# A fused linear attention and two-layer MLP on one core: the first weight tile loaded later, two chunks in the accumulators' banks, a state sum moved inside its half step, another order of the last two steps

## The chip, the core and the metric

The kernel runs on one core of a Trainium2 chip. Its time is the device time of one execution, in microseconds (us), from the launch to the last output byte. Three runs of the kernel before took 585.03, 585.46 and 587.11 us; the median, 585.46 us, is the time that the changed kernel is compared with. The names of the engines are those of the profile: PE multiplies matrices, PEld loads its weights, DVE and POOL work on tensors of elements, ACT computes functions, SP issues the DMA transfers.

## The reference

```python
gamma = 1.0 - 2.0 ** (-5.0 - np.arange(H))
for t in range(S):                       # linear attention, B=2, H=8, S=768, D=64
    state = gamma * state + k[:, :, t] outer v[:, :, t]
    y[:, :, t] = scale * q[:, :, t] @ state
x = y as (1536 tokens, 512)
h = x @ w_in;  g = max(h, 0) + alpha * min(h, 0);  x = g @ w_out       # 512 -> 2048 -> 512
h = x @ w_in2; P = a0 + a1 h + a2 h^2 + a3 h^3
Q = 1 + |b0||h| + |b1| h^2;  g = P / (Q + 1e-6);  out = g @ w_out2
```

Activations are float32, the weights are float64. All products of the MLPs are made of three matmuls of a high and a low half (x high by w high, x low by w high, x high by w low).

## The kernel before, in words

**Attention.** The 1536 tokens are 12 chunks of 128, c0 to c11, six for each batch. A chunk has two parts on PE. Its scores (`att_b`, L132, two PSUM banks sc0 and sc1) are masked on DVE into `s` (L136); `q` is scaled on ACT (L141) and, for chunks 0 to 3, on POOL (L143). Then `att_c` makes the output y of the chunk: y from `s` and v (L154), the new term of the state `st` (L166), and y from the old state R and q (L178); DVE adds `st` to R (L184), ACT and DVE split y into the halves xh (L188) and xl (L189), which are the input of the first MLP. Chunks 0 to 3 run ahead of the main loop, with 8 small matmuls (L498, two records each) ahead of the first of them; the scores of chunk 4 are behind them, and the rest of the chunks stand inside the main loop, at places that a table names (`stages`).

**MLPs.** 96 steps (`STEPS`) go over three blocks of 512 tokens and 16 tiles of 128 columns of the first and of the second MLP. Step i multiplies x by one tile of w_in (`pe_h`, L310, 12 matmuls, one PSUM bank) two steps ahead of the use, activates it, and multiplies the result by the tile of w_out into four accumulators (`pe_out`, L327, 12 matmuls). The first three products of step 0 are w high by g high, w high by g low, w low by g high.

**PSUM.** Four banks are a ring, given in turn to scores, to `h`, and to y and `st` of the chunks in the main loop (`rbank`). Four are the accumulators; the chunks ahead of the main loop use them for y and `st` (`abank`).

**Weights.** They arrive as raw 64-bit words, 512 KB a tile (L246), in the order of the list `SEQ`: k0, k1 and k2 are the first three tiles of w_in, k3 is the first tile of w_out, then they alternate. A tile is made into float32 by ACT (L254), three steps on DVE (L260, L264, L268), a cast to the high half on ACT (L279), and a subtraction to the low half on DVE (L285). `START` names the half step at which the first of these begins, and a helper, `half`, issues what falls due; at its end it issues the loads of the next tiles (`load_next`), as long as no more than 3 to 4 are under way. The half steps -12 to -5 belong to the chunks ahead of the loop, one each. `START[0,0,0]` is set by hand to -10, one earlier than the rule of its neighbours gives.

**Loads.** All loads go by SP, in program order, into one queue. Ahead of the loop: q and k transposed of a chunk (L102, L103) and k and v (L106, L107), 256 KB each; the first weight tile stands behind the first two chunks' q and k.

**The end.** In the second MLP the activation of a step is in four parts: `act2_front` (ACT: L372 to L374) and `act2_q` (DVE: L378), `act2_mid` (ACT: L385, L386; DVE: L387, L388), `act2_tail` (DVE: L396, L397, L400) and `act2_split` (ACT cast, L407; then L409). The order of the program is the order on each engine.

Of the kernel before, what the change touches and what calls it, by code (L numbers as in the profile page):

```python
# [21 lines left out]
LA = 2  # L22
NSTEP = 2 * NB * NF
QC = 1.0 + 1e-6
NWARM = 8
NSLOT = 42
GA = 5
GC = 10
# [3 lines left out]
def tile_fused(  # L32
# [18 lines left out]
    nc = tc.nc  # L51
# [49 lines left out]
    def load_kq(c):  # L101
        nc.sync.dma_start(out=att[c]["q"], in_=qT[c])  # L102
        nc.sync.dma_start(out=att[c]["t"], in_=kT[c])  # L103

    def load_nv(c):
        nc.sync.dma_start(out=att[c]["k"], in_=kn[c])  # L106
        nc.sync.dma_start(out=att[c]["v"], in_=vn[c])  # L107
# [37 lines left out]
    def att_c(c, ybank, pbank):  # L145
        a = att.pop(c)
        y = ybank(f"y{c}")
        first = c % CPB == 0
        last = c % CPB == CPB - 1
        for j in range(NK):  # L150
            js = slice(j * P, (j + 1) * P)
            for e in range(2):
                h = 2 * j + e
                nc.tensor.matmul(  # L154
                    y[64 * e:64 * e + 64, js],
                    a["v"][:, 64 * h:64 * h + 64],
                    a["s"][:, 512 * e + j * P:512 * e + (j + 1) * P],
                    start=(j == 0),
                    stop=(first and j == NK - 1),
                )  # L160
        if not last:
            pst = pbank(f"st{c}")
            for h in range(2 * NK):
                j, e = divmod(h, 2)
                hs = slice(64 * h, 64 * h + 64)
                nc.tensor.matmul(  # L166
                    pst[64 * e:64 * e + 64, 64 * j:64 * j + 64],
                    a["k"][:, hs],
                    a["v"][:, hs],
                    start=True,  # L170
                    stop=True,
                )
        if not first:
            for j in range(NK):
                js = slice(j * P, (j + 1) * P)
                for e in range(2):
                    es = slice(64 * e, 64 * e + 64)
                    nc.tensor.matmul(y[es, js], R[es, j, :], a["q"][es, js], start=False, stop=(j == NK - 1))  # L178
        if not last:
            src = pst[:, 0:256].rearrange("p (j d) -> p j d", j=NK)  # L180
            if first:
                nc.scalar.copy(R, src)
            else:
                nc.vector.tensor_tensor(out=R, in0=R, in1=src, op=ALU.add)  # L184
        b, o = divmod(c * P, TB)
        osl = slice(o, o + P)
        hap = xs(0, b, slice(0, 4), osl)
        nc.scalar.copy(hap, r4(y))  # L188
        nc.vector.tensor_tensor(  # L189
            out=xs(1, b, slice(0, 4), osl), in0=r4(y), in1=hap.bitcast(F32), op=ALU.subtract  # L190
        )
        for nm in ("qk", "kv", "s"):
            drop(a[nm])
# [27 lines left out]
    START = {}  # L221
    for m in A:
        START[0, m, 0], START[0, m, 1] = 2 * m - 9, 2 * m - 4
    START[0, 0, 0] = -10
    for j, m in enumerate(B):
        START[0, m, 0], START[0, m, 1] = 6 + (17 * j) // 5, 8 + (17 * j) // 5
    for m in range(NF):
# [12 lines left out]
    def load_next(depth):  # L240
        while loaded[0] < len(SEQ) and loaded[0] - loaded[1] < depth:
            k = loaded[0]
            loaded[0] += 1
            l, m, n = SEQ[k]
            r = alloc(f"r{k}", U32)
            nc.sync.dma_start(out=r, in_=SRC[l][n][m].bitcast(U32))  # L246
            words = r.rearrange("p (f t) -> p f t", t=2)
            raw[k] = (words[:, :, 0], words[:, :, 1], r)
# [106 lines left out]
    def act1_hi(i):  # L355
        nc.scalar.copy(g_tiles(i)[0], T1[i][1])  # L356

    def act1_lo(i):
        gh, gl = G[i]
        _, p, t = T1.pop(i)  # L360
        nc.vector.tensor_tensor(out=gl, in0=p, in1=gh.bitcast(F32), op=ALU.subtract)  # L361
        drop(t)
# [103 lines left out]
    def half(t, scalar_last=None, between=None):  # L466
        evs = dec.get(t, ())

        def each(nm):
            return [e[1] for e in evs if e[0] == nm]  # L470

        for e in each("abs"):
            w_abs(e)
        for e in each("hi"):
            w_hi(e)
        if scalar_last:
            scalar_last()
        for e in each("word"):
            w_word(e, 0)
        for e in each("lo"):  # L480
            w_lo(e)
        for e in each("word"):
            w_word(e, 1)
        if between:
            between()
        for e in each("word"):
            w_word(e, 2)
        if later and t % 2 == 0:
            split_x(*later.pop(0))
        load_next(3 if t < -6 else 4 if t < 2 * N1 else 2)  # L490

    with tc.manual_schedule():
        wt = alloc("wz")
        wz = wt[:, 0:P]
        nc.vector.memset(wz, 0.0)
        ps = rbank("warm")
        for _ in range(NWARM):
            nc.tensor.matmul(ps[:, 0:P], wz, wz, start=True, stop=True)  # L498
        nc.scalar.preload_act_table_set("natural_log_exp_and_others")
        for c in range(4):  # L500
            att_tiles(c)
        load_kq(0)
        nc.sync.dma_start(out=dm_sb, in_=dm)
        nc.sync.dma_start(out=cst_sb, in_=cst)
        load_nv(0)
        load_kq(1)
        load_next(1)
        load_kq(2)
        load_nv(1)
        nc.sync.dma_start(out=dq_sb, in_=dq)  # L510
        load_kq(3)
        load_nv(2)
        load_nv(3)
        load_next(3)
        nc.sync.dma_start(out=alpha_sb, in_=alpha)
        nc.sync.dma_start(out=ab_sb[:, 0:4], in_=pa.partition_broadcast(P))
        nc.sync.dma_start(out=ab_sb[:, 4:6], in_=pb.partition_broadcast(P))
        nc.vector.memset(bb_sb[:, 2:3], QC)

        def keep_warm(cnt):  # L520
            w = abank(3)("warm")
            for _ in range(cnt):
                nc.tensor.matmul(w[:, 0:P], wz, wz, start=True, stop=True)  # L523

        order = [("b", 0), ("c", 0), ("b", 1), ("b", 2), ("c", 1), ("b", 3), ("c", 2), ("c", 3)]
        for n, (s, c) in enumerate(order):
            if n in (1, 2, 3):
                keep_warm((3, 2, 3)[n - 1])
            if s == "b":
                att_k(c)  # L530
                att_b(c, rbank)
            else:
                att_c(c, abank(c % 2), abank(2 + c % 2))
                if c < 2:
                    att_load(4 + c)
            if n == 6:
                nc.scalar.activation(bb_sb[:, 0:2], ab_sb[:, 4:6], AF.Abs)
                nc.scalar.mul(nalpha_sb, alpha_sb, -1.0)
            half(n - NPRE)
        drop(wt)  # L540
        att_b(4, rbank)
        att_k(4)


        stages = {-4: ("c", 4)}
        for c, t, u in ((5, -3, -2), (6, -1, 1), (7, 2, 4), (8, 5, 6), (9, 7, 9), (10, 10, 12), (11, 13, 14)):
            stages[t] = ("b", c)
            stages[u] = ("c", c)

        def stage(t):  # L550
            if t not in stages:
                return
            s, c = stages[t]
            if s == "b":
                att_b(c, rbank)
                att_k(c)
            else:
                att_c(c, rbank, rbank)
                if c + 2 < NCH:
                    att_load(c + 2)  # L560
                if c == NCH - 1:
                    drop(dm_sb)

        for i in range(-LA, NSTEP):
            new, old = i + LA, i + LA - 1
            if new < NSTEP - 1:
                pe_h(new)
            if new == NSTEP - 2:
                pe_h(NSTEP - 1)
            if 0 <= old < N1:  # L570
                half(2 * i, lambda: act1_hi(old), lambda: act1_lo(old))
            else:
                if N1 <= old < NSTEP:
                    act2_tail(old)
                half(2 * i)
            if N1 <= new < NSTEP:
                act2_front(new)
                act2_q(new)
            if N1 <= old < NSTEP:
                act2_split(old)  # L580
            stage(2 * i)
            if i >= 0:
                pe_out(i)
            if i >= 0 and STEPS[i][4]:
                evac(i)
            if N1 <= new < NSTEP:
                act2_mid(new)
            stage(2 * i + 1)
            half(2 * i + 1, (lambda: act1_front(new)) if new < N1 else None)
            if new < N1:  # L590
                act1_join(new)
# [77 lines left out]
```

## Time and profile before

| | |
|---|---|
| median of three runs | 585.46 us |
| the profiled execution | 585.32 us |
| its span in the trace | 583.5 us |
| outside the span | 1.82 us |
| PE | 574.8 us busy, 99% |
| DVE | 466.3 us busy, 80% |
| ACT | 365.5 us busy, 63% |
| POOL | 76.0 us busy, 13% |

PE is busy in nearly the whole span, so what is left to gain is PE's idle time, and what can be lost is any wait that is put in front of PE. The 40 slices of the profile's page show it below full use in the first two and the last. The load queue is busy at the start: 327 to 401 GB/s in the first four slices (58 us), less than half of that afterwards.

### The profile page before, as it was taken

The page shows a single profiled execution, that of the slowest core. Times are in us where ns is not written, and L with a number is a line of the kernel's source. Part 1 is how long each engine was busy: PE and PEld are TensorE (multiplying, and loading weights), DVE is VectorE, ACT ScalarE, POOL GpSimd, SP SyncE. Part 2 cuts the span into 40 slices and gives each one's busy share as a digit, 9 for nine tenths or more (in the row PEclk, how much of TensorE's full clock was granted, in tenths as well). Part 3 has the DMA queues.
Part 4 walks back from the last instruction along what each step waited for, and adds up shares of the span by engine and source line. Part 5 has one row for each costly group of instructions (what it writes and reads, how often), then busy time and mean ns, then how long its engine had stood idle before and what let it go on. Part 6 is the DMA issues. An engine that isn't in the chain of part 4 may idle for free.

```text
span 583.5 us, 8093 instructions
## 1 busy us (share of the span) xinstructions
PE 574.8 (99%) x3040; PEld 474.6 (81%) x3040; DVE 466.3 (80%) x733; ACT 365.5 (63%) x663; POOL 76.0 (13%) x60
## 2 busy tenths in 40 slices
PE   9989999999999999999999999999999999999996
PEld 8768787888888888888888888888888888888885
DVE  3898687688684364548998999999998999887886
ACT  3676465556553453436765787777786786686672
POOL 2402000000000000000000312223222221221220
PEclk9999999999999999999999999999999999999999
DMA  9998422334321002012451011001111100010101
GB/s 327 340 401 326 145 73 73 109 109 145 108 73 36 1 37 73 36 38 90 176 204 37 0 37 37 23 15 37 36 38 37 38 0 1 0 73 2 63 9 74
DMA packets 18760, 50.65 MB, mean 87 GB/s; under 512 B 2592, under 2 KB 2592, under 8 KB 18720
## 3 DMA queue, kind: packets, MB, share of 16 engines
q1 hardware_dynamic: 18720, 50.13, 24.2%
q8 instruction: 24, 0.39, 0.3%
q14 instruction: 16, 0.13, 0.1%
HBM read 46.97 MB, written 3.15 MB: 86 GB/s over the span
## 4 chain that ended last, share of the span: by engine, by line
PE 93%; DVE 3%; ACT 2%; DMA 1%; issue 0%; ACTq 0%
PE h L310 44%; PE acc L327 43%; PE sc L132 2%; PE y L154 2%; PE y L178 1%; DMA qk<-in_qT_dram 1%; PE st L166 1%; PE warm L498 1%; DVE z L268 0%; DVE p L424 0%; PE warm L523 0%; ACT kv L120 0%; ACT g L407 0%; DVE as L400 0%; DVE z L264 0%
## 5 line engine op out<-in xcount | busy, mean ns | idle before, releaser
L310 PE MATMUL h<-xh,wh 128*128 128x512 f32 x384 | 150.3, 391 | 1.5 <-DVE xl L189 1.5
L310 PE MATMUL h<-xh,wl 128*128 128x512 f32 x384 | 149.5, 389 | 0.0
L310 PE MATMUL h<-xl,wh 128*128 128x512 f32 x384 | 149.4, 389 | 0.0
L327 PE MATMUL acc<-wh,g 128*128 128x512 f32 x384 | 125.9, 390 | 0.4 <-ACT g L407 0.4
L409 POOL TENSOR_TENSOR g<-as,g 128x512 fp32r<-128x512 f32 x46 | 63.4, 1378 | 447.9 <-PE acc L327 265.1
L327 PE MATMUL acc<-g,wh 128*128 128x512 f32 x384 | 118.9, 391 | 0.0
L310 PEld LDWEIGHTS h<-xh,wh 128*128 128x128 f32 x384 | 72.2, 188 | 17.3 <-DVE xl L189 1.7
L327 PEld LDWEIGHTS acc<-wh,g 128*128 128x128 f32 x384 | 72.0, 188 | 16.1 <-ACT g L407 0.8
L310 PEld LDWEIGHTS h<-xh,wl 128*128 128x128 f32 x384 | 72.1, 188 | 15.0
L327 PEld LDWEIGHTS acc<-g,wh 128*128 128x128 f32 x384 | 71.6, 188 | 15.6 <-issue 0.7
L310 PEld LDWEIGHTS h<-xl,wh 128*128 128x128 f32 x384 | 72.1, 188 | 14.6
L279 ACT CAST wh<-z 128x512 fp32r<-128x512 f32 x64 | 39.6, 619 | 58.4 <-DVE z L268 57.0
L327 PE MATMUL acc<-g,wl 128*128 128x512 f32 x192 | 74.7, 389 | 0.0
L327 PE MATMUL acc<-wl,g 128*128 128x512 f32 x192 | 74.7, 389 | 0.0
L351 DVE SCALAR_TENSOR_TENSOR np<-np,nalpha_sb 128x512 f32<-128x512 f32 x48 | 35.9, 748 | 39.9 <-ACT np L346 39.9
L345 ACT ACTIVATE np<-h 128x512 f32<-128x512 f32 x48 | 28.5, 594 | 45.3 <-PE h L310 45.3
L372 ACT ACTIVATE as<-h 128x512 f32<-128x512 f32 x48 | 28.6, 597 | 41.2 <-PE h L310 41.2
L378 DVE SCALAR_TENSOR_TENSOR as<-as,bb_sb,rr 128x512 f32<-128x512 f32 x48 | 37.9, 791 | 13.0 <-ACT rr L373 13.0
L361 DVE TENSOR_TENSOR g<-np,g 128x512 fp32r<-128x512 f32 x48 | 33.9, 707 | 17.4 <-ACT g L356 17.2
L268 DVE SCALAR_TENSOR_TENSOR z<-r,z 128x512 uint32<-128x512 uint32 x64 | 44.9, 701 | 1.5
L264 DVE SCALAR_TENSOR_TENSOR z<-r,z 128x512 uint32<-128x512 uint32 x64 | 44.9, 702 | 1.0
L285 DVE TENSOR_TENSOR wl<-z,wh 128x512 fp32r<-128x512 f32 x64 | 45.0, 703 | 0.1
(55 smaller groups left out, 748.3 us busy)
## 6 DMA issues: line engine op xcount, KB each, us to landing
r<-in_w1i_dram SPq DMA_DIRECT2D x16, 512.0 KB, 5.1
r<-in_w1o_dram SPq DMA_DIRECT2D x16, 512.0 KB, 3.8
r<-in_w2i_dram SPq DMA_DIRECT2D x16, 512.0 KB, 3.4
r<-in_w2o_dram SPq DMA_DIRECT2D x16, 512.0 KB, 3.2
qk<-in_qT_dram SPq DMA_DIRECT2D x12, 256.0 KB, 6.4
qk<-in_kT_dram SPq DMA_DIRECT2D x12, 256.0 KB, 6.4
kv<-in_kn_dram SPq DMA_DIRECT2D x12, 256.0 KB, 6.2
kv<-in_vn_dram SPq DMA_DIRECT2D x12, 256.0 KB, 6.5
```

Source lines behind the costliest of these rows:

```text
L264: nc.vector.scalar_tensor_tensor(out=zu, in0=lo, scalar=29, in1=zu, op0=ALU.logical_shift_right, op1=ALU.bitwise_or)
L268: nc.vector.scalar_tensor_tensor(out=zu, in0=hi, scalar=0x80000000, in1=zu, op0=ALU.bitwise_and, op1=ALU.bitwise_or)
L279: nc.scalar.copy(hi, Z[k])
L285: nc.vector.tensor_tensor(out=lo, in0=Z[k], in1=hi.bitcast(F32), op=ALU.subtract)
L310: nc.tensor.matmul(ps, w[:, ks], xs(hl, b, k, ALL), start=(n == 0), stop=(n == 11))
L327: nc.tensor.matmul(acc[0][k], a, c, start=(begin and n == 0), stop=(end != "" and n == 2))
L345: nc.scalar.activation(n, h, AF.Relu, scale=-1.0)
L351: nc.vector.scalar_tensor_tensor(out=p, in0=n, scalar=nalpha_sb[:, m:m + 1], in1=p, op0=ALU.mult, op1=ALU.add)
L361: nc.vector.tensor_tensor(out=gl, in0=p, in1=gh.bitcast(F32), op=ALU.subtract)
L372: nc.scalar.activation(s, h, AF.Square)
L378: nc.vector.scalar_tensor_tensor(out=s, in0=s, scalar=bb_sb[:, 1:2], in1=r, op0=ALU.mult, op1=ALU.add)
L409: eng.tensor_tensor(out=gl, in0=a, in1=gh.bitcast(F32), op=ALU.subtract)
```

## The change

It has six parts. (1) 7 of the small matmuls instead of 8. (2) The hand-set start of the first weight tile goes, so that its conversion begins one half step later, with chunk 1's output instead of the scores of chunk 2. (3) The loads ahead of the loop are in another order: the first weight tile behind chunk 2's k and v instead of behind chunk 1's q and k. (4) y and `st` of chunks 4 and 5 use the accumulators' banks. (5) The chunk work of an even half step (`stage(2 * i)`) is issued between the second and the third DVE step of the weight conversion instead of after the half step. (6) In the last step `act2_front` and `act2_q` of step 95 are issued ahead of `act2_tail` of step 94.

```diff
--- before.py
+++ after.py
@@ -22,7 +22,7 @@
 LA = 2
 NSTEP = 2 * NB * NF
 QC = 1.0 + 1e-6
-NWARM = 8
+NWARM = 7
 NSLOT = 42
 GA = 5
 GC = 10
@@ -221,7 +221,6 @@
     START = {}
     for m in A:
         START[0, m, 0], START[0, m, 1] = 2 * m - 9, 2 * m - 4
-    START[0, 0, 0] = -10
     for j, m in enumerate(B):
         START[0, m, 0], START[0, m, 1] = 6 + (17 * j) // 5, 8 + (17 * j) // 5
     for m in range(NF):
@@ -504,12 +503,12 @@
         nc.sync.dma_start(out=cst_sb, in_=cst)
         load_nv(0)
         load_kq(1)
+        load_nv(1)
+        load_kq(2)
+        nc.sync.dma_start(out=dq_sb, in_=dq)
+        load_nv(2)
         load_next(1)
-        load_kq(2)
-        load_nv(1)
-        nc.sync.dma_start(out=dq_sb, in_=dq)
         load_kq(3)
-        load_nv(2)
         load_nv(3)
         load_next(3)
         nc.sync.dma_start(out=alpha_sb, in_=alpha)
@@ -555,7 +554,10 @@
                 att_b(c, rbank)
                 att_k(c)
             else:
-                att_c(c, rbank, rbank)
+                if c < 6:
+                    att_c(c, abank(c % 2), abank(2 + c % 2))
+                else:
+                    att_c(c, rbank, rbank)
                 if c + 2 < NCH:
                     att_load(c + 2)
                 if c == NCH - 1:
@@ -567,18 +569,26 @@
                 pe_h(new)
             if new == NSTEP - 2:
                 pe_h(NSTEP - 1)
-            if 0 <= old < N1:
-                half(2 * i, lambda: act1_hi(old), lambda: act1_lo(old))
+            if old < N1:
+
+                def middle():
+                    if old >= 0:
+                        act1_lo(old)
+                    stage(2 * i)
+
+                half(2 * i, (lambda: act1_hi(old)) if old >= 0 else None, middle)
             else:
+                if new == NSTEP - 1:
+                    act2_front(new)
+                    act2_q(new)
                 if N1 <= old < NSTEP:
                     act2_tail(old)
                 half(2 * i)
-            if N1 <= new < NSTEP:
+            if N1 <= new < NSTEP - 1:
                 act2_front(new)
                 act2_q(new)
             if N1 <= old < NSTEP:
                 act2_split(old)
-            stage(2 * i)
             if i >= 0:
                 pe_out(i)
             if i >= 0 and STEPS[i][4]:
```

On SP, ahead of the loop: the four loads of chunk 4 (qk4, kv4), of chunk 5 (qk5, kv5) and the weight tiles r3 (k3, the first of w_out) and r4. Before:

```order
L106 DMA kv4_172<-in_kn_dram 128x512
L107 DMA kv4_172<-in_vn_dram 128x512
L246 DMA r3_227<-in_w1o_dram 128x1024
L102 DMA qk5_258<-in_qT_dram 128x512
L103 DMA qk5_258<-in_kT_dram 128x512
L106 DMA kv5_259<-in_kn_dram 128x512
L107 DMA kv5_259<-in_vn_dram 128x512
L246 DMA r4_319<-in_w1i_dram 128x1024
```

After:

```order
L106 DMA kv4_171<-in_kn_dram 128x512
L107 DMA kv4_171<-in_vn_dram 128x512
L102 DMA qk5_252<-in_qT_dram 128x512
L103 DMA qk5_252<-in_kT_dram 128x512
L106 DMA kv5_253<-in_kn_dram 128x512
L107 DMA kv5_253<-in_vn_dram 128x512
L245 DMA r3_261<-in_w1o_dram 128x1024
L245 DMA r4_318<-in_w1i_dram 128x1024
```

The load of r3 has moved from ahead of chunk 5's four loads to behind them, since by part (2) one tile fewer is finished at the half step that issued it.

On DVE, around the output of chunk 4 (`st4`, `y4`) and the mask of chunk 5 (`s5`); z2 is the pair of tiles k2 and k3 in conversion, wl0_1 the low half of k1. Before:

```order
L285 TENSOR_TENSOR wl0_1_398<-z0_199,wh0_1_397 128x512
L264 SCALAR_TENSOR_TENSOR z2_350<-r2_126,z2_350 128x512
L268 SCALAR_TENSOR_TENSOR z2_350<-r2_126,z2_350 128x512
L184 TENSOR_TENSOR R_72<-R_72,st4_415 128x256
L189 TENSOR_TENSOR xl1_79<-y4_406,xh1_76 128x4x128
L136 TENSOR_TENSOR s5_451<-sc5_0_441,dm_sb_74 128x512
L136 TENSOR_TENSOR s5_451<-sc5_1_442,dm_sb_74 128x512
```

After:

```order
L284 TENSOR_TENSOR wl0_1_397<-z0_221,wh0_1_396 128x512
L263 SCALAR_TENSOR_TENSOR z2_349<-r2_125,z2_349 128x512
L184 TENSOR_TENSOR R_72<-R_72,st4_411 128x256
L189 TENSOR_TENSOR xl1_79<-y4_402,xh1_76 128x4x128
L267 SCALAR_TENSOR_TENSOR z2_349<-r2_125,z2_349 128x512
L136 TENSOR_TENSOR s5_450<-sc5_0_440,dm_sb_74 128x512
L136 TENSOR_TENSOR s5_450<-sc5_1_441,dm_sb_74 128x512
```

R and xl1 have moved ahead of z2's third step (L268, in the new file L267).

On DVE, in the last two steps, where as94 and as95 are the activations of steps 94 and 95. Before:

```order
L388 SCALAR_TENSOR_TENSOR as94_4835<-as94_4835,ab_sb_70,h94_4805 128x512
L396 SCALAR_TENSOR_TENSOR as94_4835<-as94_4835,rr_2816 128x512
L397 SCALAR_TENSOR_TENSOR as94_4835<-as94_4835,ab_sb_70,rr_2816 128x512
L400 SCALAR_TENSOR_TENSOR as94_4835<-as94_4835 128x512
L378 SCALAR_TENSOR_TENSOR as95_4862<-as95_4862,bb_sb_71,rr_2816 128x512
L409 TENSOR_TENSOR g94_4858<-as94_4835,g94_4858 128x512
L387 TENSOR_TENSOR as95_4862<-as95_4862,h95_4818 128x512
```

After:

```order
L387 SCALAR_TENSOR_TENSOR as94_4834<-as94_4834,ab_sb_70,h94_4804 128x512
L377 SCALAR_TENSOR_TENSOR as95_4857<-as95_4857,bb_sb_71,rr_2815 128x512
L395 SCALAR_TENSOR_TENSOR as94_4834<-as94_4834,rr_2815 128x512
L396 SCALAR_TENSOR_TENSOR as94_4834<-as94_4834,ab_sb_70,rr_2815 128x512
L399 SCALAR_TENSOR_TENSOR as94_4834<-as94_4834 128x512
L408 TENSOR_TENSOR g94_4862<-as94_4834,g94_4862 128x512
L386 TENSOR_TENSOR as95_4857<-as95_4857,h95_4817 128x512
```

`act2_q` of step 95 has moved from behind `act2_tail` of step 94 (L396, L397, L400) to ahead of it.

## Rows read from the trace of the kernel before

**Rows 1.** The page's first line.

```profile
span 583.5 us, 8093 instructions
```

**Rows 2.** Waits of PE: in total us, times, longest us.

```profile
PE h L310 <- DVE xl L189: 1.5, 1, 1.5
...
PE y L154 <- DVE R L184: 0.7, 1, 0.7
PE sc L132 <- DVE R L184: 0.4, 1, 0.4
PE acc L327 <- ACT g L407: 0.4, 1, 0.4
PE y L178 <- POOL qk L143: 0.3, 1, 0.3
```

**Rows 3.** Busy time by stretch: PE, PEld, DVE, ACT, POOL, clock, DMA share, GB/s.

```profile
4.83:24.50 19.67, 18.50 (x274) 16.27 (x273) 12.28 (x20) 9.10 (x24) 9.00 (x7) 1.00 1.00 355
24.50:45.50 21.00, 19.05 (x164) 15.21 (x163) 20.20 (x37) 16.12 (x42) 0.00 (x0) 1.00 1.02 392
```

**Rows 4.** The chain that ended last, at its start: start us, us, what.

```profile
1.05 3.78 PE warm L498 x16
```

**Rows 5.** Issues of loads on SP: start us, us, then the tile.

```profile
10.44 0.33 SPq L106 DMA_DIRECT2D kv<-in_kn_dram  x1
11.13 0.33 SPq L107 DMA_DIRECT2D kv<-in_vn_dram  x1
...
21.93 0.33 SPq L246 DMA_DIRECT2D r<-in_w1o_dram  x1
...
23.74 0.43 SPq L107 DMA_DIRECT2D kv<-in_vn_dram  x1
```

**Rows 6.** The same four loads, in the same order: KB, us from issue to landing.

```profile
kv<-in_kn_dram SPq DMA_DIRECT2D x1, 256.0 KB, 5.4
kv<-in_vn_dram SPq DMA_DIRECT2D x1, 256.0 KB, 6.8
r<-in_w1o_dram SPq DMA_DIRECT2D x1, 512.0 KB, 4.2
kv<-in_vn_dram SPq DMA_DIRECT2D x1, 256.0 KB, 5.7
```

**Rows 7.** The page's queues: packets, MB, share of 16 engines.

```profile
q8 instruction: 24, 0.39, 0.3%
```

**Rows 8.** PE in order of time: start us, us, operation, idle before and releaser.

```profile
18.11 1.09 PE L154 MATMUL y<-s,kv 128*64 128x128 f32 x16 [0.66 <-DVE R L184]
...
43.08 0.39 PE L327 MATMUL acc<-g,wl 128*128 128x512 f32 x1
```

**Rows 9.** ACT, around the conversion of k3.

```profile
27.39 0.68 ACT L254 ACTIVATE z<-r 128x512 f32<-128x512 f32 x1
27.98 0.60 ACT L279 CAST wh<-z 128x512 fp32r<-128x512 f32 x1
```

**Rows 10.** DVE, from there to the low half of k3.

```profile
28.61 0.69 DVE L285 TENSOR_TENSOR wl<-z,wh 128x512 fp32r<-128x512 f32 x1
...
32.03 1.29 DVE L136 TENSOR_TENSOR s<-sc,dm_sb 128x512 f32<-128x512 f32 x2 [0.46 <-PE sc L132]
...
41.16 0.69 DVE L285 TENSOR_TENSOR wl<-z,wh 128x512 fp32r<-128x512 f32 x1
```

**Rows 11.** The end: DVE, ACT and PE in order of time.

```profile
568.59 0.69 DVE L396 SCALAR_TENSOR_TENSOR as<-as,rr 128x512 f32<-128x512 f32 x1 [0.26 <-ACT rr L386]
...
568.94 0.69 ACT L373 ACTIVATE rr<-h,bb_sb 128x512 f32<-128x512 f32 x1
...
570.59 0.74 DVE L378 SCALAR_TENSOR_TENSOR as<-as,bb_sb,rr 128x512 f32<-128x512 f32 x1
570.70 0.62 ACT L407 CAST g<-as 128x512 fp32r<-128x512 f32 x1 [0.41 <-DVE as L400]
...
571.36 0.69 DVE L409 TENSOR_TENSOR g<-as,g 128x512 fp32r<-128x512 f32 x1
...
571.96 0.68 DVE L387 TENSOR_TENSOR as<-as,h 128x512 f32<-128x512 f32 x1
...
576.12 0.50 PE L327 MATMUL acc<-wh,g 128*128 128x512 f32 x1 [0.43 <-ACT g L407]
```

## The prediction

> **What bounds the kernel now.** I read the page's first lines, then the waits of PE, then the busy time by stretch, and only then single instructions. The profiled execution took 585.32 us, of which the span is 583.5 [rows 1]; 1.82 us lie outside. Its time is 0.14 below the median of the runs, 585.46, so a sum made on it stands for the median less 0.14. PE's waits [rows 2] show how little it waits once the loop runs: the named ones come to 1.5 + 0.7 + 0.4 + 0.4 + 0.3 = 3.3 us. So a change can gain only about that, and the question is which of these waits go and what is late next. Both start stretches tell what is late next [rows 3]: from 4.83 to 24.50 us the load queue is full (DMA share 1.00) and PE has 1.17 of 19.67 us idle; from 24.50 to 45.50 us the loads are still full and DVE is busy 20.20 of 21.00 us, while PE is idle for 1.95. In the second stretch DVE, not PE, sets the pace: a PE that waits less there arrives earlier at an operand that DVE makes. The TensorE clock is granted in full in both rows, so it is no term.
>
> **The change, ahead of the loop.** One small matmul of eight goes: 16 records take 3.78 us [rows 4], so 0.47 us each. PE's wait for POOL's scaled q of chunk 1, 0.3 [rows 2], is also likely to go, since chunk 1's k and v and chunk 2 come earlier. PE is then ready for the scores of chunk 3 some 0.8 us earlier. But its transposed k no longer comes where it did. The queue works in order and without a gap, so I let a landing go with its place in the queue, counted in bytes. By that chunk 3's q and k, behind r0's 512 KB, take the places of chunk 2's k and v. Those were issued at 10.44 and 11.13 [rows 5] and took 5.4 and 6.8 us [rows 6]: landings 15.84 and 17.93. Chunk 3's scores can therefore not start before some 17.9, as against 16.29 in the trace of before (the y of chunk 2 that waits 0.66 us is right behind them and starts at 18.11 [rows 8]); the y of chunk 2 then comes about 1.0 us later than it did. If the long step between the two landings, 17.93 − 15.84 = 2.1, does not fall there, the landing is at 16.5 and nothing is lost. Bounds for the start of the first `h`: 0 to +0.8 us. I take +0.8, the row's own landing; it costs little in the end, because the loop's first steps wait for DVE anyway (below).
>
> The Trainium skill bears on that long step ("Runtime: NRT & Kernel Launch", section "Instruction fetch mechanics"): each engine's sequencer fetches its program in blocks of 16 KiB by a DMA queue of its own while it executes, at a cost that is mostly hidden. The page of the profile has such a queue with 24 packets and 0.39 MB, that is 16 KB each [rows 7], so the size agrees; hidden it is not quite, if such a fetch is what took the 2.1 us step against some 0.7 for its neighbours, which the rows do not prove. By the rule the cost falls at a place of the program and not of the load queue, and could fall on another tile; that is a rival below.
>
> **The banks (part 4).** Chunk 5's scores wait 0.4 us for DVE's R of chunk 4, and the `h` of step 2 waits 1.5 us for DVE's xl of chunk 5 [rows 2], each because its ring bank is still read. In the accumulators y and `st` hold no ring bank, so both waits go. The accumulators are first used by the loop at the first `pe_out`, after chunk 5's output has been read, so I price the other side at 0. For PE alone this would be −1.9. PE reaches the third matmul of the first `pe_out` (w low, L327) at 43.08 [rows 8]; without the 1.5 it would be there at 41.5. But this operand is the low half of k3, and DVE makes that at 41.16, done 41.85 [rows 10]. So PE could gain 1.2 before it met DVE, if DVE stayed as it was.
>
> **The load of k3 (parts 2 and 3).** It doesn't. SP now issues k3 behind chunk 5's four loads. Its place in the queue is then that of chunk 5's v: 512 KB more ahead than before in q, k, k, v of 256 KB each, less its own. It landed at 21.93 + 4.2 = 26.1; chunk 5's v landed at 23.74 + 5.7 = 29.4 [rows 5, 6]. So k3 lands at 29.4 (28.7 to 30.0, one load of 256 KB to either side). ACT took it up at 27.39 without a wait [rows 9]. Now ACT stands at it for 29.4 − 27.4 = 2.0 us, and behind it on ACT is the cast of k1's high half, for which DVE's low half of k1 (28.61 [rows 10], 1.22 after ACT's start) waits. DVE begins that at 29.4 + 1.25 = 30.65. Ahead of chunk 5's mask five DVE instructions stand, 28.61 to 31.57 (32.03 less the 0.46 idle), that is 2.96 us at most and 2.8 if the overlaps stay: the mask starts at 33.5 instead of 32.03, 1.45 later. From there to the low half of k3 DVE is busy without a gap, 41.16 − 32.03 = 9.13 [rows 10]; the same instructions stand there after the change. So the low half of k3 starts at 42.6 and is done at 43.3, and PE's third matmul comes at 43.3 instead of 43.08: **+0.25**. Bounds: k3 at 28.7 gives −0.4, k3 at 30.0 gives +0.85. The gain of the banks is thus paid back by a load that is 3.3 us later. Later tiles take their old places in the queue (the bytes ahead are the same), so I price the rest of the program at 0.
>
> **The state sum (part 5).** R and xl of an even half step now stand ahead of one DVE instruction of 0.69 us (L268). On chunk 4 this makes them 0.69 earlier, while nothing waits for R any more than y of chunk 5, which comes later; the instruction that is put back is done before the mask in either order. I take 0, with bounds of ±0.3 that lie inside those of k3.
>
> **The end (part 6).** `act2_q` of step 95 (L378) now stands on DVE ahead of `act2_tail` of step 94. It needs ACT's Abs of step 95, 568.94 + 0.69 = 569.63 [rows 11]. So DVE, which began L396 of step 94 at 568.59, now waits until 569.66 and begins it after L378, whose place to the next start is 0.67: 569.66 + 0.67 = 570.33, **1.74 later**. Is any of it won back? Before, L378 ran from 570.59 to 571.33, beside ACT's cast of step 94 (570.70 to 571.32), for which DVE's L409 waited anyway. That hole is empty now. So L409 and behind it L387 of step 95 (571.96) come 1.74 later too, and from there a chain of DVE, the cast and PE leads to the last `pe_out`, which already waits 0.4 us for it (576.12) [rows 2, 11]. No cover: it comes at 577.86, and the output behind it in the same measure. Bounds: 0.67, if Abs of step 95 came before DVE was free, and 1.74; Abs stands behind the Exp of step 94 on ACT, which L396 itself waited for, so I take 1.74.
>
> **Sum:** 585.32 + 0.25 + 1.74 = 587.3 us.
>
> **Rivals.** *The banks' gain stands.* k3 is in time or DVE has room: PE gains at most the 1.9 of the two waits, −1.6 after the late start of the loop, and the end gives 1.74 back: 585.5. For it: PE's waits are the only ones named in the stretch. Against it: DVE is busy 20.20 of 21.00. *The end costs nothing.* ACT's work of step 95 is early enough: 585.32 + 0.25 = 585.6. Against it stand the two times 568.94 and 568.59. With both, 585.32 − 1.6 = 583.7 and with the small matmul 583.3; faster by over 0.5% (below 582.5) needs yet another us. *Slower: the long step falls in front of k3.* The long step of 2.1 instead of some 0.7 us moves from chunk 2's v to the tiles ahead of k3; k3 lands 1.45 later, at 30.85, and from there every us goes through DVE to the third matmul: 587.3 + 1.45 = 588.8. It decides from a landing of about 30.3. For it: one such step is in the rows and the change moves PE against the queue; against it: in before the loads from 21.93 to 29.4 hold no such step. *The load order does not do what it says:* the weight tile behind chunk 2 leaves chunk 3's k to wait; that is in the forecast.
>
> **How the numbers follow.** Forecast 0.65, with a range of its own of 586.7 to 587.9 (−0.4 and +0.85 for k3 in place of +0.25). The banks' gain stands 0.12; the end is free 0.08; the long step in front of k3 0.15. The range 585.3 to 588.8 reaches over the first two to the price of the third. A measurement of this kernel can tell about 0.5%, 2.9 us, from no change: faster means below 582.5, slower above 588.4. Faster needs both faster rivals and more: 0.04. Slower: the long step, and the far end of the forecast: 0.18. Same: 0.78.
>
> **What would show it.** Right: k3's Abs on ACT at about 29.4 after a wait of 2 us for the load; chunk 5's mask at 33.5; no wait of `h` for xl, and in its place a wait of the third matmul of the first `pe_out` for the low half of k3, near 43.3; L396 of step 94 waits for L378, and PE waits about 2.2 us ahead of its last 12 matmuls. Wrong: k3 lands before 28, or PE's third matmul is before 42.5, or the last `pe_out` starts less than a us later against the steps ahead of it.

## The result, and the profile after

The changed kernel took 589.02 us (median of 8 runs, 587.83 to 589.47), the kernel before 585.43 us beside it. The ratio, which goes by all runs, is 1.0053, 95% interval 1.004 to 1.0065: slower by 3.1 us (2.3 to 3.8), 588.5; the two medians are 3.6 apart. The prediction said 1.8 us slower, 587.3. The profiled execution took 589.17 us with a span of 587.4, 3.9 more than [rows 1].

The waits of PE in the changed kernel (in total us, times, longest us):

```profile
PE sc L132 <- DMA qk<-in_kT_dram: 2.2, 1, 2.2
PE y L154 <- DMA kv<-in_vn_dram: 1.8, 1, 1.8
PE acc L326 <- ACT g L406: 1.6, 2, 1.5
PE acc L326 <- DVE wl L284: 1.1, 1, 1.1
```

The two waits that the banks were to remove [rows 2] are gone. In their place stand a load (chunk 3's transposed k), a DVE operand at the first `pe_out`, and a longer wait at the end. The second row is the y of chunk 0, whose v landed at 8.36 instead of 7.13; by chunk 2's scores 0.29 us of that is left (12.59 instead of 12.30). Where PE waits for the load, the busy times by stretch (PE, PEld, DVE, ACT, POOL, granted clock, DMA share, GB/s) show something that no row of before held:

```profile
4.83:24.50 19.67, 15.60 (x222) 14.02 (x222) 9.15 (x16) 8.01 (x21) 8.23 (x7) 0.91 1.00 357
16.20:18.50 2.30, 0.06 (x2) 0.03 (x1) 1.94 (x4) 0.71 (x2) 0.54 (x1) 1.00 1.02 389
18.50:20.39 1.89, 1.89 (x16) 1.67 (x16) 0.89 (x2) 1.12 (x3) 1.36 (x1) 0.55 1.05 347
20.39:22.13 1.74, 1.74 (x18) 1.74 (x19) 1.29 (x2) 1.65 (x4) 1.15 (x1) 0.51 1.01 342
22.13:24.50 2.37, 2.37 (x50) 2.13 (x48) 0.48 (x2) 0.68 (x3) 0.12 (x1) 1.00 0.91 277
```

The first row answers to the first of [rows 3], where the clock was 1.00. PE stands almost still from 16.20 to 18.50 us; in the two stretches behind it the granted clock is 0.55 and 0.51, the lower of its two levels (1.2 GHz), and from 22.13 us it is whole again (2.4 GHz). PE in order of time shows the price:

```profile
18.50 1.96 PE L132 MATMUL sc<-qk 64*128 64x128 f32 x16 [2.25 <-DMA qk<-in_kT_dram]
20.39 1.90 PE L154 MATMUL y<-s,kv 128*64 128x128 f32 x16
...
23.71 1.09 PE L154 MATMUL y<-s,kv 128*64 128x128 f32 x16
...
26.22 1.16 PE L132 MATMUL sc<-qk 64*128 64x128 f32 x16
27.31 0.50 PE L309 MATMUL h<-xh,wh 128*128 128x512 f32 x1
...
44.98 0.50 PE L326 MATMUL acc<-g,wl 128*128 128x512 f32 x1 [1.15 <-DVE wl L284]
```

The y of chunk 2 starts at 20.39 instead of 18.11 [rows 8] and takes 1.90 us; the same form at full clock takes 1.09, two rows on. The third matmul of the first `pe_out` is at 44.98 instead of 43.08 [rows 8], 1.90 later. What it waits for is DVE's work, here from the first conversion step behind chunk 3's xl, over the low half of k1 and chunk 5's mask, to the low half of k3; the last row is ACT's first step on k3:

```profile
27.56 0.42 DVE L259 TENSOR_SCALAR z<-z 128x512 uint32<-128x512 uint32 x1
...
31.69 0.69 DVE L284 TENSOR_TENSOR wl<-z,wh 128x512 fp32r<-128x512 f32 x1
...
35.12 1.28 DVE L136 TENSOR_TENSOR s<-sc,dm_sb 128x512 f32<-128x512 f32 x2
...
44.24 0.68 DVE L284 TENSOR_TENSOR wl<-z,wh 128x512 fp32r<-128x512 f32 x1
...
30.47 0.68 ACT L253 ACTIVATE z<-r 128x512 f32<-128x512 f32 x1
```

Each of the last three on DVE is 3.08 or 3.09 later than its row of before (28.61, 32.03, 41.16 [rows 10]). The whole chain has moved, and it was late before k3 was wanted: ACT took up k3 at 30.47 without a wait, and k3 had landed at 29.84.

The end, DVE and PE:

```profile
571.71 0.75 DVE L377 SCALAR_TENSOR_TENSOR as<-as,bb_sb,rr 128x512 f32<-128x512 f32 x1 [1.33 <-ACT rr L372]
572.38 0.68 DVE L395 SCALAR_TENSOR_TENSOR as<-as,rr 128x512 f32<-128x512 f32 x1
...
579.96 0.50 PE L326 MATMUL acc<-wh,g 128*128 128x512 f32 x1 [1.46 <-ACT g L406]
```

DVE stands 1.33 us for ACT's Abs of step 95, and L395 of step 94 is 3.79 later than in [rows 11], PE's last group 3.84. So the sum of the 3.9 us is: 3.08 late on DVE, less the 1.23 us that the low half of k3 had in hand (done at 41.85, used at 43.08), some 0.2 by which the broken-up group runs longer, and the rest, 1.8, at the end.

This profile does not stand for every run. The mean granted clock of each run is on record: 0.995 to 0.996 in three of the eight, the profiled one among them (588.88 to 589.20 us), and 1.000 in the other five (587.83, 587.96, 588.44, 589.37 and 589.47). In the profiles of all the kernels here, a mean of 0.997 or less goes with a stretch at the lower level in the first 38 us, and a mean of 0.998 or more with none. So in those five the clock did not fall as shown above, and still their median is 3.0 us above the kernel before; two of them were the slowest of the eight. They have no trace; by which path they lost is not shown.

### The profile page after: what moved, and what is told of

It is laid out like the page before. It is cut to its first block, busy times and chain, and to the rows that moved or that the text cites. A ratio compares the mean times of both kernels' runs of the same rounds, so it can differ in the third digit from the quotient of the medians.

```text
span 587.4 us, 8084 instructions
## 1 busy us (share of the span) xinstructions
PE 575.3 (98%) x3038; PEld 474.1 (81%) x3038; DVE 465.2 (79%) x733; ACT 365.5 (62%) x663; POOL 74.6 (13%) x60
## 4 chain that ended last, share of the span: by engine, by line
PE 92%; DVE 3%; DMA 2%; ACT 1%; SPq 1%; issue 0%; ACTq 0%
PE h L309 43%; PE acc L326 43%; PE y L154 2%; PE sc L132 1%; PE y L178 1%; DMA qk<-in_kT_dram 1%; DMA kv<-in_vn_dram 1%; PE st L166 1%; DVE p L423 0%; DVE s L136 0%; ACT g L406 0%; DVE as L399 0%; DVE as L396 0%; DVE z L263 0%; DVE z L267 0%
## 5 line engine op out<-in xcount | busy, mean ns | idle before, releaser
L267 DVE SCALAR_TENSOR_TENSOR z<-r,z 128x512 uint32<-128x512 uint32 x64 | 46.0, 718 | 1.5
L263 DVE SCALAR_TENSOR_TENSOR z<-r,z 128x512 uint32<-128x512 uint32 x64 | 44.0, 687 | 1.0
```

Of the source, the lines that this page charges most:

```text
L263: nc.vector.scalar_tensor_tensor(out=zu, in0=lo, scalar=29, in1=zu, op0=ALU.logical_shift_right, op1=ALU.bitwise_or)
L267: nc.vector.scalar_tensor_tensor(out=zu, in0=hi, scalar=0x80000000, in1=zu, op0=ALU.bitwise_and, op1=ALU.bitwise_or)
```

## The experiments

Two theories on the middle. *Theory 1:* the start sets the loss; chunk 3's late load and the lower clock delay DVE's chain. *Theory 2*, the prediction's: a late start is hidden behind DVE, and the late k3 sets the loss. The times are medians; ratios are to the kernel before, which took 585.45 to 585.68 us beside them.

**The end, part 6.** First alone on the kernel before, then undone in the changed kernel:

```diff
+                if new == NSTEP - 1:
+                    act2_front(new)
+                    act2_q(new)
                 if N1 <= old < NSTEP:
                     act2_tail(old)
                 half(2 * i)
-            if N1 <= new < NSTEP:
+            if N1 <= new < NSTEP - 1:
```

> The kernel before with part 6 alone (act2_front and act2_q of step 95 ahead of act2_tail of step 94). Theory 1 (DVE stands until Abs of step 95 is done, and nothing behind it has slack): 1.74 us more than before, 587.2 to 587.4 us; L396 of step 94 at 570.3 instead of 568.6 and PE's wait ahead of its last twelve matmuls 0.4 + 1.7 us less what PE itself loses on step 94. Rival (most of it is covered by PE's last matmuls of step 94): 586.2 us or less.

587.15 us, ratio 1.0027 (1.0016 to 1.0038): 1.6 us slower.

> The changed kernel with the old order of the last two steps. Theory 1 (the end costs what the sum of the prediction said): 1.74 us less than the changed kernel, 587.3 us; L395 of step 94 starts right behind the Exp of step 94 again, and PE waits about 0.4 us ahead of its last twelve matmuls. Rival (the end costs only what PE's waits grew by in the profile of the changed kernel, 1.46 + 0.17 - 0.43 = 1.2 us): 587.8 us. The wait of the first pe_out for the low half of k3 (1.1 us) stays in both.

586.74 us, ratio 1.0009 (0.9996 to 1.0022), 2.3 below the changed kernel; 0.5 more than expected, and in its profile the start came 0.9 us earlier too (third matmul at 44.04). DVE and PE of the run with part 6 alone:

```profile
569.70 0.75 DVE L378 SCALAR_TENSOR_TENSOR as<-as,bb_sb,rr 128x512 f32<-128x512 f32 x1 [1.32 <-ACT rr L373]
570.37 0.69 DVE L396 SCALAR_TENSOR_TENSOR as<-as,rr 128x512 f32<-128x512 f32 x1
...
577.95 0.50 PE L327 MATMUL acc<-wh,g 128*128 128x512 f32 x1 [1.42 <-ACT g L407]
```

L396 starts at 570.37 instead of 568.59 and PE's last group at 577.95 instead of 576.12 [rows 11]. The rivals, 1.2 or less, fall by these rows and by the 2.3 of the run with part 6 undone; the time of part 6 alone (0.9 to 2.2) would leave room for 1.2. PE's waits alone undercount, because step 94's group is late as well (0.18 us of wait there, and its ends).

**The banks, part 4, and the state sum, part 5.** The banks alone on the kernel before, then with part 5:

```diff
-                att_c(c, rbank, rbank)
+                if c < 6:
+                    att_c(c, abank(c % 2), abank(2 + c % 2))
+                else:
+                    att_c(c, rbank, rbank)
```

> The kernel before with one part of the change alone: y and st of chunks 4 and 5 in the accumulators' banks. Theory 1 (both waits of PE go, and PE then meets DVE's low half of k3 at 41.4 to 41.9): the third matmul of the first pe_out at 41.4 to 41.9 instead of 43.08, 583.8 to 584.3 us. Rival (DVE is the bound of the stretch, so PE's waits only move): 585.4 us. Second rival (the accumulators' first use waits for the readers of chunk 5's output): slower than 585.4.

584.07 us, ratio 0.9964 (0.9951 to 0.9978). PE meets DVE at the third matmul, as expected:

```profile
41.41 0.50 PE L327 MATMUL acc<-g,wl 128*128 128x512 f32 x1 [0.51 <-DVE wl L285]
```

> The kernel before with parts 4 and 5: the banks and the state sum, and all 8 small matmuls. Beside the run with parts 1, 4 and 5 (584.58 us, 584.1 to 587.4) and the banks alone (584.07). Theory (part 5 moves nothing that PE waits for, and the 8th small matmul fills PE's time at the start, where the loads are the bound): 584.0 us within 0.3, with none of 12 runs above 586. Rival (part 5 costs the 0.5): 584.6 us.

584.75 us, ratio 0.9984 (0.9976 to 0.9993); none of 11 runs above 585.67. The time is the rival's, not the theory's. By the times alone it could be the start: in this profile, the longest of the 11 runs, PE stood 1.97 us for POOL's scaled q, and the first `h` came at 25.61 instead of 24.54 in the banks alone. The rows show part 5's own share. DVE around the state sum, the banks alone:

```profile
29.29 0.68 DVE L264 SCALAR_TENSOR_TENSOR z<-r,z 128x512 uint32<-128x512 uint32 x1
30.01 0.69 DVE L268 SCALAR_TENSOR_TENSOR z<-r,z 128x512 uint32<-128x512 uint32 x1
30.62 0.41 DVE L184 TENSOR_TENSOR R<-R,st 128x256 f32<-128x256 f32 x1
30.95 0.68 DVE L189 TENSOR_TENSOR xl<-y,xh 128x512 fp32r<-128x512 f32 x1
31.55 1.28 DVE L136 TENSOR_TENSOR s<-sc,dm_sb 128x512 f32<-128x512 f32 x2
```

and with part 5 as well:

```profile
30.61 0.68 DVE L264 SCALAR_TENSOR_TENSOR z<-r,z 128x512 uint32<-128x512 uint32 x1
31.60 0.42 DVE L184 TENSOR_TENSOR R<-R,st 128x256 f32<-128x256 f32 x1 [0.31 <-PE y L178]
32.22 0.69 DVE L189 TENSOR_TENSOR xl<-y,xh 128x512 fp32r<-128x512 f32 x1 [0.20 <-ACT xh L188]
32.83 0.68 DVE L268 SCALAR_TENSOR_TENSOR z<-r,z 128x512 uint32<-128x512 uint32 x1
33.43 1.28 DVE L136 TENSOR_TENSOR s<-sc,dm_sb 128x512 f32<-128x512 f32 x2
```

The same five rows take 2.26 us to the start of the mask (29.29 to 31.55) and 2.82 (30.61 to 33.43); in the changed kernel, too, it is 2.82. R can't come earlier, because the y of the chunk reads the old R; put ahead of L268, it makes DVE stand for PE, and xl for ACT. L268 had filled just that time. Part 5 costs 0.56 us of DVE in a stretch that DVE bounds, about what the banks gave DVE there: in the kernel before, the mask stood 0.46 us for the scores [rows 10].

**The place of k3, parts 2 and 3.** First k3 early in the changed kernel, then k3 late in the kernel with the banks. `load_next` at the end of the half step -9 gets another depth (4 in the first, 2 in the second):

```diff
-        load_next(3 if t < -6 else 4 if t < 2 * N1 else 2)
+        load_next(4 if t == -9 else 3 if t < -6 else 4 if t < 2 * N1 else 2)
...
+        load_next(2 if t == -9 else 3 if t < -6 else 4 if t < 2 * N1 else 2)
```

> The changed kernel with k3 issued ahead of chunk 5's four loads, as in the kernel before; all else as changed. Theory 1 (the start sets the time; ACT takes up k3 at 30.47 though it landed at 29.84): k3 lands near 27, and nothing else moves: 589.0 us within 0.3. Theory 2 (the late k3 sets it): the third matmul of the first pe_out 1.3 to 1.9 us earlier, 587.1 to 587.7 us.

588.37 us (586.14 to 589.13), ratio 1.0027 (1.001 to 1.0044). The median is within theory 1's bounds but for 0.3, the scatter is not. In its profile, 589.12 us, chunk 3's k lands at 18.26, k3 at 27.25, and the third matmul is at 44.87: with the start late, the place of k3 moves nothing. Four of the 12 runs lie at 586.1 to 586.7, with a mean clock of 0.999 or 1.000; the five at 588.82 to 589.13, the profiled one among them, have 0.995 or 0.996. So without the low clock this kernel can be some 2.5 us faster than in its profile. A run of 588.73 had 1.000, and those at 586 us have no trace: whether chunk 3's k came in time there is not shown.

> The kernel before with part 4 (the banks), and k3 issued behind chunk 5's four loads as in the changed kernel; the start and the end as before. It measures by itself the term that the prediction put at the middle. Theory (the late k3 holds ACT's cast and DVE's low half of k1, and from there DVE is busy without a gap; it was only hidden in the changed kernel, whose start was later still): k3 lands near 29.5, the third matmul of the first pe_out comes at 42.9 to 43.4 instead of 41.4, 585.6 to 586.1 us, 1.5 to 2.0 above the banks alone. Rival (the place of k3 never matters): 584.1 us.

586.71 us, ratio 1.0017 (1.0008 to 1.0026), 2.6 above the banks alone, more than the 1.5 to 2.0 expected. ACT and then DVE in order of time:

```profile
30.47 0.67 ACT L254 ACTIVATE z<-r 128x512 f32<-128x512 f32 x1 [2.04 <-DMA r<-in_w1o_dram]
31.05 0.60 ACT L279 CAST wh<-z 128x512 fp32r<-128x512 f32 x1
...
31.68 0.69 DVE L285 TENSOR_TENSOR wl<-z,wh 128x512 fp32r<-128x512 f32 x1 [2.27 <-ACT wh L279]
```

k3 landed at 30.45, a us later than expected: a landing step of 1.69 us instead of some 0.67 stands in the queue ahead of it (chunk 5's transposed k at 26.83, its k at 28.52). ACT stands 2.04 us for it, DVE 2.27 for the cast behind, and the low half of k3 is at 43.67. So the prediction's mechanism exists, with a price. The start of this profile was 0.6 us later than that of the banks alone (first `h` at 25.16 instead of 24.54); the two stands for k3 show that k3, not the start, was the later of the two.

**The start, parts 1 to 3.** The old load order in the changed kernel (the diff of the load order backwards):

> The changed kernel with the old order of the loads ahead of the loop; k3 still stands behind chunk 5's loads. Theory 1 (the start: chunk 3's transposed k lands at 18.4, PE stands 2.25 us, its clock falls, and DVE's chain behind it is 3.1 us late): scores of chunk 3 near 16.2 at a granted clock of 1.00, first h near 24.5 instead of 27.3; then k3, landing near 29.4, binds, and the third matmul of the first pe_out comes at 43.3 to 43.7 instead of 44.98: 587.3 to 587.7 us. Theory 2 (the prediction's: a late start is hidden behind DVE, and k3 sets the time): the third matmul where it is, 589.0 us.

589.68 us, ratio 1.0058 (1.0039 to 1.0077). Neither theory fits: in the profile (590.32 us) chunk 3's scores are back at 17.06 at full clock, and the time is not better. Something else is late, the mask of chunk 3, for which PE waits 2.3 us, and behind that wait the clock falls again (granted 0.50 from 23.03 to 25.20 us). DVE and PE, then busy times from 18.40 us here and from 17.55 in the changed kernel:

```profile
18.40 0.85 DVE L259 TENSOR_SCALAR z<-z 128x512 uint32<-128x512 uint32 x1
19.28 1.41 DVE L263 SCALAR_TENSOR_TENSOR z<-r,z 128x512 uint32<-128x512 uint32 x1
20.73 1.64 DVE L267 SCALAR_TENSOR_TENSOR z<-r,z 128x512 uint32<-128x512 uint32 x1
22.30 1.28 DVE L136 TENSOR_TENSOR s<-sc,dm_sb 128x512 f32<-128x512 f32 x2
...
23.03 2.35 PE L154 MATMUL y<-s,kv 128*64 128x128 f32 x15 [2.30 <-DVE s L136]
...
18.40:22.30 3.90, 2.33 (x48) 2.02 (x44) 3.83 (x5) 1.20 (x3) 3.34 (x3) 1.00 1.01 350
...
17.55:19.42 1.87, 0.92 (x10) 0.95 (x12) 1.80 (x4) 0.20 (x1) 0.46 (x1) 0.80 1.04 408
```

The later start of tile 0 (part 2) puts its three steps between chunk 1's xl and chunk 3's mask, and there each takes about twice its usual 0.42, 0.69 and 0.69 us, while POOL is busy 3.34 of the 3.90 us from 18.40 to 22.30. In the changed kernel the same steps run at 17.55 to 19.42, with POOL busy for 0.46, in 1.87 us. The Trainium skill ("SBUF — State Buffer", section "Who interferes with whom") says that DVE and GpSimd (POOL) share a pair of ports, and that a DVE instruction with two inputs in SBUF contends for it with a GpSimd instruction that reads SBUF. L263 and L267 have two such inputs, and the trace agrees in kind. L259 has one and doubled as well; the section names its operation, `tensor_scalar`, among those that can contend in a two-port mode, and no run here shows whether L259 ran in one. No run changes POOL alone, so POOL as the cause rests on the overlap. In this profile, then, part 2 makes chunk 3 late without part 3; part 3 without part 2 was not run. Part 3 undone does not bring the time back even without the low clock: five of the ten runs have a mean of 0.999 or 1.000 and took 587.50 to 589.39 us, the five at 0.995 to 0.997 took 589.98 to 590.96. Parts 2 and 3 both undone (parts 1, 4, 5 and 6 stay):

> The changed kernel with both the old start of the first weight tile and the old order of the loads (parts 2 and 3 undone; 7 small matmuls, banks, state sum and new end order stay). Theory 1 (either of parts 2 and 3 alone makes chunk 3 late and lowers the clock; with both undone the start is that of before): third matmul of the first pe_out at 41.3 to 41.9, so the gain of the banks, 1.6 us, and the loss of the end, 1.74, are left: 585.5 to 586.0 us, 3.0 to 3.5 below the changed kernel. Theory 2 (the start costs nothing by itself, and only k3's place counts): 587.1 to 587.7 us.

586.36 us, ratio 1.0017 (1.0006 to 1.0027), 2.7 below the changed kernel: theory 1, 0.4 above its bounds, which held part 5 for free. Its profile fell on its slowest run, 589.24 us, and stands for none of the others: there the clock fell at the very start, behind a stand of 1.82 us for chunk 0's v (granted 0.54 from 8.62 to 12.30 us, mean 0.995), while the other eleven runs have a mean of 0.998 or more.

Then more small matmuls in front of chunk 3's scores, to keep PE busy where it stood for the transposed k:

> The changed kernel with 6 more small matmuls of its own kind (about 0.29 us each, 1.75 us) in front of chunk 3's scores, where PE stands 2.25 us for the transposed k. Theory 1 (the stand of PE lets the granted clock fall to 0.51 to 0.55 for the scores of chunk 3 and the y of chunk 2, 1.96 and 1.90 us instead of 1.16 and 1.09, and DVE's chain carries that to the first pe_out): both groups at 1.00 again, first h at 25.7 instead of 27.3; of these 1.6 us the third matmul of the first pe_out gets 0.6 to 1.6 (k3 lands at 29.8 and binds next): 587.4 to 588.4 us. Rival (the clock is low there for another reason, or DVE hides it): 589.0 us.

```diff
+            if n == 5:
+                keep_warm(6)
```

587.74 us (587.46 to 588.27), ratio 1.0039 (1.0027 to 1.0051), 1.3 less than the changed kernel. It is inconclusive on the clock, since in its profile the long landing step missed chunk 3's transposed k (landed at 15.92), so that PE had nothing to bridge. But it shows what the changed kernel does when its start is on time. DVE and PE:

```profile
30.75 0.69 DVE L284 TENSOR_TENSOR wl<-z,wh 128x512 fp32r<-128x512 f32 x1 [1.69 <-ACT wh L278]
...
33.49 1.28 DVE L136 TENSOR_TENSOR s<-sc,dm_sb 128x512 f32<-128x512 f32 x2
...
42.62 0.68 DVE L284 TENSOR_TENSOR wl<-z,wh 128x512 fp32r<-128x512 f32 x1
...
43.35 0.50 PE L326 MATMUL acc<-g,wl 128*128 128x512 f32 x1 [1.51 <-DVE wl L284]
```

The prediction had these at 30.65, 33.5, 42.6 and 43.3. Then parts 1 to 3 alone on the kernel before:

> The kernel before with parts 1, 2 and 3 alone: 7 small matmuls, the first weight tile one half step later, the new load order. Theory 1 (chunk 3's scores wait for their transposed k, the clock falls, DVE begins k1's conversion 3.1 us later, at 27.5, and from there to the low half of k3 it takes 16.69 us as before): third matmul of the first pe_out near 45.0 instead of 43.08, 587.2 to 587.6 us. Theory 2 (the prediction's: the late start is hidden, and k3's place costs 0.25): 585.5 to 585.9 us.

588.55 us, ratio 1.0056 (1.0042 to 1.007): as much as the whole change, and more than either theory said. Its profile took another path. ACT, then PE:

```profile
30.35 0.67 ACT L253 ACTIVATE z<-r 128x512 f32<-128x512 f32 x1 [2.81 <-DMA r<-in_w1o_dram]
...
33.96 1.73 PE L132 MATMUL sc<-qk 64*128 64x128 f32 x14 [3.33 <-DVE R L184]
...
46.41 0.39 PE L326 MATMUL acc<-g,wl 128*128 128x512 f32 x1
```

Here chunk 3's k landed in time (16.93; first `h` at 24.66, only 0.2 late), so theory 1 has no ground; k3 landed at 30.32, 2.48 us behind chunk 5's v at 27.84, where a tile of 512 KB usually takes 1.28. ACT stands 2.81 for k3, DVE's R of chunk 4 comes late behind it, and since without the banks chunk 5's scores need that R's bank, PE stands 3.33 us. Behind that stand the clock falls once more (14 of the records take 1.73 us instead of 1.16). So the traces show two ways in which the new load order can lose 2 to 3 us: the long landing step on chunk 3's k, or one in front of k3.

**What is left over.** Parts 1, 4 and 5, and then the banks with the four low-half products of the first `pe_out` issued last:

> Parts 1, 4 and 5 alone: 7 small matmuls, the banks, the state sum; the old start, load order and end. Theory 1: the gain of the banks alone, 583.8 to 584.3 us; PE's start 0.4 earlier is lost at the next landing, and the state sum moves nothing that PE waits for. Rival: part 5 lets DVE finish xl earlier and the low half of k3 later, by 0.3 us either way.

584.58 us (584.14 to 587.41), ratio 0.9992 (0.998 to 1.0004): with part 5 known to cost, the rest is the banks' gain. The two runs at 587.26 and 587.41 are the only ones with a mean clock of 0.997, the others have 0.999 or more.

```diff
+            todo += [(k, n, a, c) for n, (a, c) in enumerate(prs)]
+        if i == 0:
+            todo.sort(key=lambda e: e[1] == 2)
```

> The kernel before with the banks, and in the first pe_out the four products with the low half of k3 as the last four instead of the third of each three. Theory (that operand is what PE meets next, 0.5 us of wait in the banks alone): the wait goes, 583.5 to 583.7 us, 0.3 to 0.6 below the banks alone, and less scatter. Rival (DVE's next low half is late in its place): 584.1 us.

582.60 us (582.37 to 583.3), ratio 0.9952 (0.9939 to 0.9964): 2.9 below the kernel before and 6.4 below the changed one. All that PE still waits for, beside its own start:

```profile
PE y L154 <- DMA kv<-in_vn_dram: 1.4, 1, 1.4
...
PE acc L331 <- ACT g L411: 0.4, 1, 0.4
PE y L178 <- POOL qk L143: 0.4, 1, 0.4
```

No wait for a low half is left; its gain over the banks alone, 1.5, is above the 0.3 to 0.6 expected. The two profiles are 1.23 apart (582.60 and 583.83), and 0.55 of that is the start (first `h` at 23.99 instead of 24.54), which this change does not touch; the wait that is gone was 0.51, and the rest is the group of matmuls that is no longer broken up. So some 0.7 is its own.

## Why the prediction was right or wrong

- **The end, +1.74: right.** L396 of step 94 came at 570.37 against 570.33 worked out, and the end alone cost 1.6 us (0.9 to 2.2). Only the sign for it was off: PE waits 1.42 to 1.46 us ahead of its last 12 matmuls and not 2.2, since step 94's own group is late already.
- **The start of the loop, "I take +0.8 ...; it costs little in the end, because the loop's first steps wait for DVE anyway": this step failed**, twice, in the profile of the changed kernel. In size: the first `h` was 2.83 late, 27.31 instead of 24.48. The load was priced nearly right (18.37 against 17.9), but behind a stand of 2.25 us the clock fell, which made two groups 0.8 us longer each; "it is no term" was read from a row in which PE had no such stand. And in kind: DVE was taken for a cover, but DVE's chain begins with chunk 3's xl, which is made of the late y. A chain that starts from the late thing hides nothing; only the 1.23 us that its last operand had in hand did. The clock's part belongs to the three runs in which it fell. The five at full clock have a median of 588.44, 1.1 above the forecast; which term they missed stays open.
- **The late k3, +0.25: the mechanism was right, and hidden.** With the start on time (the run with more small matmuls) the four times came as worked out (within 0.1). In the changed kernel's profile it was not the later of the two paths, so the signs named for it did not show: no wait of ACT for k3, the mask at 35.12 instead of 33.5, the third matmul at 44.98 instead of 43.3. Its upper bound was too low: k3 landed at 30.3 to 30.45 in two other kernels, because a long step did fall in front of it, as the rival said. One stood there already in the trace of before, which the prediction took to hold none: chunk 5's k landed at 28.74, 1.28 behind its transposed k.
- **The banks: right.** 1.6 us by the medians (1.3 to 2.9 by the ratio), up to the meeting with DVE.
- **The state sum, 0: wrong, 0.56 us on DVE.** "This makes them 0.69 earlier" overlooked that R waits for the y that reads it.
- **The sum.** 0.25 + 1.74 said, about 2.0 + 1.8 found in the profiles; the middle was mis-sized by some 1.8. The direction was right. The size lies outside the forecast's own range, 586.7 to 587.9. That 588.5 is still under the outer bound, 588.8, is luck: that bound is the price of k3 at 30.85 with the start on time, and in the profile k3 landed at 29.84 and held up nothing. The median, 589.02, lies above it.

## What to carry to other kernels

Before calling a busy engine a cover for a late start, look up where its own chain begins: if that is the late operand, the delay passes through whole. A wait of PE for a load is priced with what the granted clock may do behind it, and a moved load with the longest landing step that the queue shows, put right in front of it. An instruction ahead of one that waits is often the filler of that wait; changing places with it adds the wait. And a profile stands for the runs that went as it did: here the mean granted clock of each run tells that the traced path was taken by three of eight.

## What the runs showed of the hardware

In every one of the 14 traces one landing step takes 1.5 to 2.2 us instead of some 0.67. It ends at 15.2 to 19.0 us, and 2.2 to 2.7 us after the start of a 16 KB packet of the instruction queue that itself takes 1.0 to 1.1 us (in the changed kernel at 16.17, chunk 3's k at 18.37). Which load it hits differs from program to program: the constants for q (`dq_sb`), chunk 3's q, its transposed k or its normal k, or chunk 2's v. That the packet causes the step is not shown; no run took it away, and the step of 2.48 us in front of k3 in the run with parts 1 to 3 alone has no such packet beside it (none starts between 22.40 and 32.44 us).

The granted clock fell to its lower level behind stands of PE of 1.82, 2.19, 2.21, 2.25, 2.30 and 3.33 us in the first 38 us, and did not behind stands of 1.83 (changed kernel, before 8.50), 1.92 (the banks with k3 late) and 1.97 us (the banks with part 5). So the length of a stand alone does not tell whether the clock falls.
